# Infini-attention with a SiLU feed-forward layer on one core: constants behind the norms, split transposes, one load on another queue, and a new list of work

## The chip, the cores and the metric

The kernel runs on one core of one Trainium2 chip. The metric is the device time of one execution in microseconds (us), as the median of several runs. The engines are TensorE (PE: matmuls; PEld: its weight loads), VectorE (DVE), ScalarE (ACT), GpSimd (POOL) and SyncE (SP, which here only issues DMAs). "L724" is line 724 of the kernel before.

## The reference

The input x is 2048 x 512, bf16. A layer norm feeds two branches, whose sum is added to x.

```python
xn = layernorm(x)
# A: 32 heads of 16, 4 segments of 512 rows, with a memory M, z carried between them
q, k, v = xn @ wq, xn @ wk, xn @ wv
phi = lambda t: where(t > 0, t + 1, exp(t))
for s in range(4):
    p = softmax(qs @ ks.T * 16**-0.5 + causal mask)
    a_dot = p @ vs
    a_mem = (phi(qs) @ M) / (phi(qs) @ z + 1e-6)
    o = g * a_mem + (1 - g) * a_dot          # g = sigmoid(beta), one per head
    M += phi(ks).T @ vs;  z += sum(phi(ks))
A = concat(o) @ wo
# B: feed-forward, inner width 1792
B = silu(xn @ w1) @ w2
out = x + A + B
```

## The kernel before

Everything runs as one flat program. A string, ORDER, lists 1349 words; a loop at the end of the kernel calls one small function (a "piece") for each word, in this order. Each engine carries out its own instructions in the order in which the words issue them, and waits only where an operand, or a buffer, is not ready. A word names the piece and its indices: `v0.1.2` is part 2 of the value product of segment 0, row tile 1. The list is thus the whole schedule: no loop over tiles or segments sets it.

The x rows come in 16 tiles of 128. The first four are loaded one by one (`load_x`, L158), tiles 0 and 2 from SyncE's queue and 1 and 3 from ScalarE's; the other tiles and the weights follow from SyncE's, except w2 and wo, which `lw0` and `lw1` load from ScalarE's (L169).

The head of the list, for tiles 0 to 3, goes tile by tile. `xc`: VectorE's statistics (L286); `xd`: their mean and variance (L289); `xq`: ScalarE's root (L303); `xi`: VectorE's reciprocal (L306); `Nv`: the normalised tile xn_t (L315); `X`: four transposes on TensorE into one PSUM bank, ptr (`turn_mm`, L845); `Xa`/`Xv`: copies of that bank into xnT by ScalarE or VectorE (`turn_copy`, L851), two copies of two blocks for tiles 0 and 1, one copy for the others. From tile 4 on, `xs` is both statistics, `xg` is root and reciprocal for four tiles on GpSimd (L297, and a power, L300), and `XD` transposes by DMA. `busy44` and `busy6` are matmuls on zeros that keep TensorE running (L864). `tb` loads ScalarE's table for the exponential.

VectorE's constants are words too: `odd` (pm_odd and pm_even, L223, L224), `omask` (L235), `bmask`, and `kind` (five small instructions, L239 to L246). They are needed by the first split of keys (odd), by the first merge of odd heads (omask), by the gate (kind) and by the memory's mask (bmask). Before the list VectorE zeroes zraw (L188) and lows (L262).

Products (`k`, `q`, `v`, `h`, `n`, `o`) accumulate in banks of a pool of four (`bank`, tag "pb"); a copy gives the bank back: `kv`/`ka`, `qv`/`qa`, `vv`/`va` by VectorE or ScalarE, `ha` (ScalarE's tanh, L492) and `hv` (VectorE, L497) for the feed-forward. `product` uses the whole 128x128 array (L336), or four column tiles of 32 (L338) where the next tiled word needs columns.

Attention comes in 72 batches, `S0` to `S71`, 18 for a segment, in the list's own order (S0 S2 S1 S3 S4 S7 S5 S11 S6 ...). A batch is a set of score matmuls into psS, four banks at once, of which there is a single copy (L724); ScalarE's exp out of psS (L730); and GpSimd's causal selects on the weights (L744). The next batch's scores can start only when the exp before has emptied psS. Batches S0 to S4 need the key tiles' split copies: `kf` (VectorE and ScalarE, for the first), `kp` (GpSimd, L385). `E`n and `O`n multiply the weights of column tile n with the values (L791), and need the selects of all their batches: E0 those of S0, S1 and S4. `Ev`/`Ov` copy the result and give back the bank; SyncE then moves the sums of the weights by DMA into zraw. `Om` merges.

`fp` (GpSimd, L417), `fa` (ScalarE) and `fv` (VectorE, L433) make phi of the keys, `gp`, `ga`, `gv` that of the queries. `tanh` (ScalarE, L249) and `gate` make the gate. `o`, `oc`, `od` add up the output, `st` stores it; for the last tile `oh` and `sh` do so in two halves.

Of the kernel before, what the change touches and what calls it, by code (L numbers as in the profile page):

```python
# [19 lines left out]
S1 Nv5 XD5 h0.0.2 h0.0.3 ha0.0 hv0.0 h0.1.0 h0.1.1 fp0.2 h0.1.2 h0.1.3 q0.2.0  # L20
S3 q0.2.1 q0.2.2 q0.3.0 q0.3.1 q0.3.2 q0.2.3 Nv7 qv0.2 ha0.1 h0.2.0 h0.2.1 kp0.2 q0.3.3
S4 qv0.3 hv0.1 XD7 fv0.2 fa0.3 h0.2.2 v0.3.0 v0.3.1 v0.3.2 t0.0 t0.2 xs10 h0.3.0 h0.3.1 h0.3.2 h0.4.0 fp0.3 h0.3.3 ha0.3 v0.3.3
S7 vv0.3 fp0.1 hv0.3 h0.4.1 h0.4.2 h0.4.3 kp0.3 h0.2.3 v1.2.0 ha0.4 v1.2.1 xs13 tanh E0 Ev0
S5 v1.2.2 v1.2.3 h0.5.0 hv0.4 h0.5.1 h0.5.2 ha0.2 h0.5.3 vv1.2 fv0.3 O0 Ov0
S11 lw0 hv0.2 xs11 q1.1.0 q1.1.1 q1.1.2 v1.1.0 v1.1.1 v1.1.2 v1.1.3 q1.1.3 q1.2.0 lw1
S6 vv1.1 q1.2.1 q1.2.2 q1.2.3 v1.3.0 v1.3.1 v1.3.2 qv1.1 ga1.1 xs8 qv1.2 v1.0.0 v1.0.1 xs9 xg8.4 v1.0.2 v1.0.3 vv1.0 v1.3.3 ha0.5 hv0.5 t0.3
S8 h0.6.0 h0.6.1 h0.6.2 gp1.1 h0.6.3 ha0.6 fv0.1 q1.0.0 q1.0.1 q1.0.2 E1
S9 vv1.3 q1.0.3 h0.7.0 h0.7.1 Ev1 hv0.6 h0.7.2 h0.7.3 ha0.7 h0.8.0 h0.8.1 h0.8.2 xs15 k1.3.0
S10 qv1.0 t0.1 hv0.7 k1.3.1 k1.3.2 k1.3.3 kv1.3 h0.8.3 fa1.3 Nv8 O1 Nv10 Ov1 q1.3.0 XD8 ha0.8 hv0.8 k1.2.0 k1.2.1 k1.2.2
S13 q1.3.1 q1.3.2 Nv9 q1.3.3 qv1.3 k1.2.3 Nv11 XD11 h0.9.0 h0.9.1 Om1 h0.9.2 h0.9.3 h0.10.0 ha0.9 hv0.9 kv1.2 kp1.2  # L30
S12 k1.0.0 k1.0.1 h0.10.1 h0.10.2 h0.10.3 k1.1.0 k1.1.1 XD9 k1.0.2 k1.0.3 ha0.10 gv1.1 kv1.0 hv0.10 kp1.0
S15 k1.1.2 h1.0.0 h1.0.1 h1.0.2 k1.1.3 h1.0.3 ha1.0 xs14 E2 kv1.1 XD10 Ev2
S17 O2 Ov2 h1.10.0 h1.10.1 h1.10.2 kp1.1 xl0.2 m0.2 mv0.2 h1.10.3 m0.0 ha1.10 mv0.0 hv1.0 fp1.3
S21 hv1.10 h0.11.0 h0.11.1 h0.12.0 h0.11.2 h0.11.3 h0.12.1 h1.3.0 ha0.11 h0.12.2 h0.12.3
S14 ha0.12 xs12 k2.1.0 hv0.11 Om0 gp1.0 h1.3.1 k2.1.1 kv2.1 hv0.12 q2.1.0 q2.1.1
S16 xg12.4 k2.2.0 k2.2.1 h1.3.2 h0.13.0 qv2.1 kv2.2 h1.3.3 Om2 E3 ha1.3
S19 h0.13.1 hv1.3 h0.13.2 h0.13.3 kp2.2 Ev3 O3 ha0.13 Ov3 v2.1.0 v2.1.1 vv2.1
S24 hv0.13 o0.2.7 oc0.2.10.1 od0.2.11.2 fv1.3 h1.8.0 h1.8.1 Nv15 XD15 h1.8.2 h1.8.3 h1.11.0 h1.11.1 h1.11.2 ha1.8
S18 hv1.8 xl0.0 o0.2.6 h1.11.3 ha1.11 o0.2.8 q2.3.0 q2.3.1 h1.1.0 h1.1.1 Nv14 qv2.3 hv1.11
S22 sv0 h1.1.2 h1.1.3 ha1.1 o0.2.2 k2.0.0 k2.0.1 oc0.2.5.0 od0.2.11.0 o0.0.13 od0.0.0.0  # L40
S20 kv2.0 hv1.1 o0.0.10 v2.2.0 v2.2.1 vv2.2 r0.0 o0.0.11 oc0.0.2.1 t1.3 E4 Ev4 ga1.0 kp1.3
S28 gp1.2 o0.2.3 r0.3 od0.2.11.3 r0.1 od0.0.0.3 r0.2 gate o0.2.1 w0 z0.3 z0.1 h1.7.0 h1.7.1 h1.7.2 h1.7.3 q2.0.0 ha1.7 oc0.0.7.0
S26 hv1.7 z0.0 oc0.0.2.0 o0.0.3 o0.0.8 q2.0.1 z0.2 fa1.1 qv2.0 o0.2.4 o0.0.12 O4
S23 h1.4.0 oc0.0.7.1 o0.2.9 o0.0.6 h1.4.1 o0.0.1 Nv12 Ov4 h1.4.2 h1.4.3 ha1.4 od0.0.0.1 o0.0.4 bmask gv1.0 od0.0.0.2
S25 h1.9.0 h1.9.1 kp2.1 Om3 zv0.3 h1.9.2 XD12 h1.9.3 ha1.9 oc0.2.10.0 hv1.4 o0.2.12 XD14 E5 zv0.1 o0.2.15
S29 xl1.1 Ev5 fp1.1 xl0.3 o0.2.17 o0.2.13 oc0.2.5.1 O5 hv1.9 mw0.0 zv0.0 ga1.2 k2.3.0 Ov5 k2.3.1 kv2.3
S27 o0.0.14 o0.0.15 o0.2.0 h1.2.0 zv0.2 h1.2.1 h1.2.2 h1.2.3 ha1.2 Om4 o0.0.17 hv1.2 o0.0.16
# [28 lines left out]
S57 h2.1.1 ha2.1 o1.1.12 oc1.1.10.0 o1.3.10 oc1.3.3.0 o1.1.11 o1.3.11 gv3.0 o1.1.4 hv2.1 o1.3.15
S54 od1.3.9.0 o1.1.8 ga3.1 o1.3.17 kp3.3 o1.1.0 od1.1.6.2 h3.11.0 o1.3.1 o1.1.2 h3.11.1 st1.3 ha3.11 od1.1.6.3 gp3.3 st1.1 O12 hv3.11
S59 o2.2.11 oc2.2.1.1 gp3.1 E12 fill Ev12 Ov12 dv2.3 h3.7.0 h3.7.1 d2.1 o2.2.2 oc2.2.6.0 ha3.7
S60 o2.0.2 o2.2.5 o2.0.7 h3.12.0 h3.12.1 hv3.7 ha3.12 o2.0.1 dv2.0 n2.0
S62 od2.2.13.1 zv2.0 nv2.0 o2.0.12 oc2.0.5.0 oc2.0.13.0 z2.3 o2.0.9 gv3.1 hv3.12 h3.1.0 h3.1.1 o2.0.10 o2.2.9 ha3.1 z2.1  # L80
# [862 lines left out]
```

## Time and profile before

| | us |
|---|---|
| median of 3 runs | 221.3 (220.81 to 221.44) |
| the profiled execution's own time | 220.8 |
| its span in the trace | 219.1 |
| TensorE busy | 211.6 (97%) |
| ScalarE busy | 184.2 (84%) |
| VectorE busy | 181.0 (83%) |
| GpSimd busy | 126.8 (58%) |

The granted clock of TensorE in the trace is 1.00 from end to end. The span begins shortly before the first instruction and ends with the last DMA of the output; 1.7 us of the profiled execution lie outside it. All times inside the trace are counted from the span's start. In the rows of the timeline the first number is the start, the second the duration; what stands in brackets is how long the engine was idle before, and what ended that. A row "x44" is a group of 44 instructions in a row. In the groups by line the two numbers behind the bar are the time busy in all (us) and the mean of one (ns).

### The profile page before, as it was taken

What the parts mean: (1) busy time and instruction counts of PE and PEld (TensorE: products, weight loads), DVE (VectorE), ACT (ScalarE), POOL (GpSimd) and SP (SyncE); (2) the same over time, 40 slices, a digit from 0 to 9 for tenths busy, and PEclk for the clock granted to TensorE, in tenths of its full rate; (3) what the DMA queues carried; (4) which work ended last, traced back from release to release, by engine and by line L of the source; (5) the groups of instructions that cost most, each with busy time, mean ns of one, the idle gap of its engine ahead of it and who ended that gap; (6) DMA issues with size and microseconds to landing.
All of it is one profiled execution on the core that took longest, in us unless ns stands there. A gap on an engine that the chain in (4) does not pass through costs nothing.

```text
span 219.1 us, 9343 instructions
## 1 busy us (share of the span) xinstructions
PE 211.6 (97%) x4019; PEld 116.3 (53%) x4042; DVE 181.0 (83%) x370; ACT 184.2 (84%) x173; POOL 126.8 (58%) x203
## 2 busy tenths in 40 slices
PE   7999999999999999999999999999999999999994
PEld 7666655556544544445544445455454544465663
DVE  7899999999897878757988979777899798669364
ACT  3899989999999999999999999999999988860000
POOL 6039986679687845695845486667768473410000
PEclk9999999999999999999999999999999999999999
...
GB/s 197 357 372 128 79 129 344 42 79 46 4 4 75 25 86 71 83 62 29 51 74 61 43 121 28 47 79 7 4 99 75 75 76 45 97 60 76 97 52 97
DMA packets 33273, 19.60 MB, mean 89 GB/s; under 512 B 14672, under 2 KB 33232, under 8 KB 33232
## 3 DMA queue, kind: packets, MB, share of 16 engines
q1 hardware_dynamic: 30608, 16.39, 29.1%
...
q14 instruction: 10, 0.08, 0.1%
...
## 4 chain that ended last, share of the span: by engine, by line
PE 82%; DVE 9%; POOL 4%; issue 2%; ACT 1%
PE ps L336 20%; PE psO L338 16%; PE ps L338 15%; PE psS L724 9%; PE psO L336 9%; PE psV L791 8%; PE psS L338 4%; DVE stats L286 2%; POOL Pb L744 2%; DVE Vz L406 1%; POOL k L385 1%; DVE hT L497 1%; DVE pk L433 1%; POOL lows L744 1%; PE ptr L845 1%
## 5 line engine op out<-in xcount | busy, mean ns | idle before, releaser
L730 ACT ACTIVATE Pb<-psS 128x2048 bf16<-128x2048 f32 x72 | 135.2, 1877 | 6.3 <-PE psS L724 4.1
L744 POOL TENSOR_SCALAR_AFFINE_SELECT Pb<-Pb 128x512 bf16<-128x512 bf16 (+2 forms) x88 | 61.6, 710 | 19.2 <-ACT Pb L730 16.5
L497 DVE SCALAR_TENSOR_TENSOR hT<-th,ps 128x512 bf16<-128x512 bf16 x56 | 38.0, 681 | 10.6 <-ACT th L492 10.2
L744 POOL TENSOR_SCALAR_AFFINE_SELECT lows<-Pb 64x512 bf16<-64x512 bf16 (+1 forms) x40 | 23.2, 581 | 37.5 <-ACT Pb L730 31.1
L338 PE MATMUL psO<-w_sb,hT 128*32 128x512 bf16 (+2 forms) x708 | 43.3, 321 | 0.0
L336 PE MATMUL ps<-xnT,w_sb 128*128 128x512 bf16 (+1 forms) x165 | 34.2, 329 | 0.4 <-DVE Vz L406 0.2
L492 ACT ACTIVATE th<-ps 128x512 bf16<-128x512 f32 x56 | 33.2, 594 | 1.7 <-PE ps L338 1.6
L338 PEld LDWEIGHTS <-hT 128*32 128x32 bf16 x876 | 21.6, 97 | 14.0 <-issue 2.6
L338 PE MATMUL ps<-xnT,w_sb 128*32 128x512 bf16 (+1 forms) x448 | 26.4, 348 | 0.0
L724 PE MATMUL psS<-qT,k 32*128 32x64 bf16 (+3 forms) x512 | 23.0, 233 | 0.5 <-ACT Pb L730 0.3
L336 PEld LDWEIGHTS <-w_sb 128*128 128x128 bf16 x168 | 15.8, 98 | 11.4 <-issue 1.0
L791 PE MATMUL psV<-Pb,Vz 128*32 128x448 bf16 (+7 forms) x512 | 21.6, 286 | 0.2 <-POOL Pb L744 0.2
L724 PEld LDWEIGHTS <-k 32*128 32x128 bf16 x512 | 9.4, 92 | 22.8 <-issue 22.2
L336 PE MATMUL psO<-w_sb,hT 128*128 128x512 bf16 (+2 forms) x82 | 20.9, 326 | 0.6 <-issue 0.5
L791 PEld LDWEIGHTS <-Vz 128*32 128x32 bf16 x768 | 16.2, 97 | 9.2 <-issue 0.8
L621 DVE SCALAR_TENSOR_TENSOR o_out<-psO,x_res 128x512 bf16<-128x512 f32 x14 | 9.6, 689 | 6.6 <-PE psO L338 4.9
L338 PEld LDWEIGHTS <-w_sb 128*32 128x32 bf16 x448 | 11.2, 96 | 7.3 <-issue 1.6
L724 PE MATMUL psS<-qT,kT 16*128 16x448 bf16 (+3 forms) x256 | 14.7, 269 | 0.0
L821 DVE CAST oraw<-psV 128x512 bf16<-128x512 f32 x15 | 10.2, 682 | 3.1 <-PE psV L791 3.0
L406 DVE CAST Vz<-ps 128x512 bf16<-128x512 f32 x15 | 10.2, 682 | 2.8 <-PE ps L338 1.6
L336 PEld LDWEIGHTS <-hT 128*128 128x128 bf16 x89 | 7.8, 98 | 8.7 <-issue 2.2
L336 PE MATMUL ps<-xnT,wq_sb 128*128 128x256 bf16 (+1 forms) x59 | 12.1, 322 | 0.2 <-issue 0.2
...
## 6 DMA issues: line engine op xcount, KB each, us to landing
...
```

Of the source, the lines that this page charges most:

```text
L286: nc.vector.bn_stats(out=stats[t][:], in_=xs(t, t + 1)[:, 0, :])
L336: return [nc.tensor.matmul(out, lhsT=lhsT, rhs=rhs, start=start, stop=stop, skip_group_check=True)]
L338: nc.tensor.matmul(out[c : c + 32], lhsT=lhsT[:, c : c + 32], rhs=rhs, start=start, stop=stop, tile_position=(0, c), skip_group_check=True,)
L406: copy(out=Vzs[s % 2][:, j, :, 0:3:2, :], in_=sts[s].pop(("v", j))[:, :].rearrange("p (h r d) -> p h r d", r=2, d=DH),)
L492: nc.scalar.activation(out=th[:], in_=sts[s]["h", ft][:, :], func=AF.Tanh, scale=0.5)
L497: nc.vector.scalar_tensor_tensor(out=st["hT"][:, ft, :], in0=st.pop(("th", ft))[:], scalar=1.0, in1=st.pop(("h", ft))[:, :], op0=ALU.add, ...
L621: out = nc.vector.scalar_tensor_tensor(out=o_out[:], in0=st.pop(("psO", j)), scalar=0.5, in1=st["x", j][:], op0=ALU.mult, op1=ALU.add)
L724: nc.tensor.matmul(psS[:, g, c : c + q2 - q1], lhsT=keys[rows], rhs=st["qT"][rows, dt, q1:q2], start=True, stop=True, tile_position=(32 * ...
L730: exp = nc.scalar.activation(out=blocks(Pb, b).rearrange("p y g c -> p g y c"), in_=psS[:, :, :].rearrange("p g (y c) -> p g y c", c=BLOCK ...
L744: over[id(Pb)].append(nc.gpsimd.affine_select(out=out, in_=in_, compare_op=ALU.is_ge, fill=0.0, base=base, pattern=[[0, out.shape[1]], [1, ...
L791: nc.tensor.matmul(psV[32 * g : 32 * g + 32, q0 : q0 + nq].rearrange("p (y c) -> p y c", y=weights.shape[2]), lhsT=Vzs[s % 2][:, kt, 4 * d ...
L821: copy(out=oraw[:], in_=sts[s].pop(("psV", 0))[:, :])
```

## The change

Four edits, and a new list.

1. The constants move in the list: `odd` behind tile 3's copy, `bmask` ahead of phi of the first key tile, `omask` and `kind` behind S0. Before, kind, odd and omask were its first three words.
2. `turn_mm` and `turn_copy` use two banks for tiles 0 and 1, two transposed blocks in each, so that each copy has a bank of its own. Before, both copies read one bank.
3. Tile 2 of x is loaded from ScalarE's queue. SyncE's issues one load fewer ahead of the weights.
4. The column split of the last tile's two halves is written as a table, LAST_COLS, with the same 256 and 256 columns.
5. The list keeps its words (four copies change engine: kv0.1 becomes ka0.1, qa3.2 and qa3.3 become qv3.2 and qv3.3, Ev14 becomes Ea14), and most stand elsewhere. The batches keep their order. Cut to the code and the first stretches:

```diff
-    load_x(nc.scalar, 1, 1)
-    load_x(nc.sync, 2, 1)
-    load_x(nc.scalar, 3, 1)
+    for t in range(1, TPS):
+        load_x(nc.scalar, t, 1)
...
-        width = D if half is None else D // 2
-        first = 0 if half is None else half * width
+        first, width = (0, D) if half is None else LAST_COLS[half]
...
+    LAST_COLS = ((0, 2 * P), (2 * P, 2 * P))
...
+    def turn_parts(t):
+        return 2 if t < 2 else 1
+
     def turn_mm(t, n):
-        ptr = xn["ptr", t] = bank([P, DT, n, P], BF16, "ptr")
-        for i in range(n):
-            xn_t = xn.pop(t + i)
-            for dt in range(DT):
-                nc.tensor.transpose(ptr[:, dt, i, :], xn_t[:, dt * P : (dt + 1) * P], ident[:])
+        parts = turn_parts(t)
+        size = DT // parts
+        xns = [xn.pop(t + i) for i in range(n)]
+        ptrs = xn["ptr", t] = []
+        for part in range(parts):
+            ptr = bank([P, size, n, P], BF16, "ptr")
+            for i in range(n):
+                for d in range(size):
+                    dt = part * size + d
+                    nc.tensor.transpose(ptr[:, d, i, :], xns[i][:, dt * P : (dt + 1) * P], ident[:])
+            ptrs.append(ptr)
...
```

The list before, to S6:

```
kind odd omask ones0 ones1 zeros xc0 xd0 xc1 xq0 xi0 Nv0 busy44 xd1 xq1 xc2 xi1 X0.1 Nv1 xd2 Xa0.1 busy6 v0.0.0 v0.0.1 xq2 X1.1 Xa1.1 xs3 xi2 Nv2 v0.0.2 xq3 v0.0.3 xi3 v0.1.0 v0.1.1 Nv3 X2.1 va0.0 k0.0.0 k0.0.1 tb Xv2.1 X3.1 v0.1.2 v0.1.3 Xv3.1 vv0.1 k0.1.0 k0.0.2 k0.0.3 ka0.0 fp0.0 kf0.0 q0.0.0 q0.0.1 q0.0.2 q0.0.3 xs4 k0.1.1 qa0.0 k0.1.2 k0.1.3 kv0.1 fa0.0 xs7
S0 k0.3.0 fa0.1 k0.2.0 k0.2.1 k0.2.2 k0.2.3 kv0.2 k0.3.1 k0.3.2 q0.1.0 xs5 xs6 xg4.4 fv0.0 k0.3.3 kv0.3
S2 q0.1.1 v0.2.0 kp0.1 q0.1.2 q0.1.3 qv0.1 v0.2.1 v0.2.2 v0.2.3 vv0.2 fa0.2 Nv6 Nv4 XD6 XD4 h0.0.0 h0.0.1
S1 Nv5 XD5 h0.0.2 h0.0.3 ha0.0 hv0.0 h0.1.0 h0.1.1 fp0.2 h0.1.2 h0.1.3 q0.2.0
S3 q0.2.1 q0.2.2 q0.3.0 q0.3.1 q0.3.2 q0.2.3 Nv7 qv0.2 ha0.1 h0.2.0 h0.2.1 kp0.2 q0.3.3
S4 qv0.3 hv0.1 XD7 fv0.2 fa0.3 h0.2.2 v0.3.0 v0.3.1 v0.3.2 t0.0 t0.2 xs10 h0.3.0 h0.3.1 h0.3.2 h0.4.0 fp0.3 h0.3.3 ha0.3 v0.3.3
S7 vv0.3 fp0.1 hv0.3 h0.4.1 h0.4.2 h0.4.3 kp0.3 h0.2.3 v1.2.0 ha0.4 v1.2.1 xs13 tanh E0 Ev0
S5 v1.2.2 v1.2.3 h0.5.0 hv0.4 h0.5.1 h0.5.2 ha0.2 h0.5.3 vv1.2 fv0.3 O0 Ov0
S11 lw0 hv0.2 xs11 q1.1.0 q1.1.1 q1.1.2 v1.1.0 v1.1.1 v1.1.2 v1.1.3 q1.1.3 q1.2.0 lw1
```

The list after, to S6:

```
ones0 ones1 zeros xc0 xd0 xc1 xq0 xi0 Nv0 busy44 xd1 xq1 xc2 xi1 X0.1 Nv1 xd2 Xa0.1 busy6 X1.1 xq2 v0.0.0 v0.0.1 v0.0.2 Xa1.1 v0.1.0 v0.1.1 xs3 xq3 xi2 Nv2 v0.0.3 X2.1 xi3 Nv3 v0.1.2 X3.1 v0.1.3 Xv2.1 k0.0.0 tb k0.0.1 Xv3.1 odd k0.0.2 vv0.1 va0.0 k0.0.3 ka0.0 kf0.0 q0.0.0 xs4 xs7 q0.0.1 q0.0.2 q0.0.3 k0.1.0 qa0.0 bmask k0.1.1 k0.1.2 fa0.0 fp0.0 fv0.0 t0.0
S0 omask kind k0.2.0 k0.2.1 xs6 xs5 xg4.4 k0.1.3 ka0.1 fp0.1 v0.2.0 v0.2.1 v0.2.2 q0.1.0 q0.1.1 q0.1.2 kp0.1
S2 v0.2.3 fa0.1 k0.2.2 k0.2.3 k0.3.0 k0.3.1 kv0.2 k0.3.2 k0.3.3 q0.1.3 vv0.2 qv0.1 kv0.3 kp0.3 Nv6
S1 h0.0.0 h0.0.1 h0.0.2 h0.0.3 XD6 h0.3.0 ha0.0 v0.3.0 v0.3.1 Nv5 XD5 v0.3.2 h0.1.0
S3 Nv4 h0.1.1 h0.1.2 hv0.0 v0.3.3 vv0.3 h0.3.1 h0.3.2 XD4 h0.3.3 h0.2.0 ha0.3 h0.1.3 xs10 hv0.3
S4 fv0.1 h0.2.1 h0.2.2 q0.3.0 q0.3.1 q0.3.2 q0.3.3 Nv7 q0.2.0 fp0.3 q0.2.1 q0.2.2 q0.2.3 ha0.1 XD7 t0.1 fa0.2 qv0.3
S7 hv0.1 h0.4.0 qv0.2 h0.4.1 h0.4.2 h0.2.3 ha0.2 h0.4.3 kp0.2 xs9 fp0.2 E0 Ev0 v1.2.0
S5 tanh v1.2.1 v1.2.2 hv0.2 xs11 v1.2.3 v1.1.0 v1.1.1 vv1.2 h0.5.0 v1.1.2 v1.1.3 vv1.1 ha0.4 hv0.4 xs8 xg8.4 h0.5.1
S11 h0.5.2 h0.5.3 ha0.5 O0 q1.1.0 Ov0 q1.1.1 q1.1.2 q1.1.3
```

Behind that, lw0 stands behind S6 and lw1 behind S14 (both behind S11 before), and VectorE's Om3, sv0, the recips r0 and w0 stand in the stretches of S18 and S22.

More of the change, by code (lines that the diff above doesn't have):

```diff
@@ L20 @@
[L20 to L47, printed above, removed]
@@ L76 @@
[L76 to L80, printed above, removed]
@@ new lines @@
+S11 h0.5.2 h0.5.3 ha0.5 O0 q1.1.0 Ov0 q1.1.1 q1.1.2 q1.1.3
+S6 k1.2.0 k1.2.1 qv1.1 k1.2.2 ga1.1 hv0.5 lw0 fv0.2 v1.3.0 v1.3.1 q1.2.0 v1.3.2 v1.3.3 vv1.3 k1.2.3 kv1.2 Nv8 XD8 q1.0.0
+S8 Nv10 q1.2.1 q1.2.2 q1.2.3 fa0.3 t0.2 h0.6.0 h0.6.1 h0.6.2 Nv11 q1.0.1 XD11 gate qv1.2 h0.6.3 E1 Ev1 ha0.6 hv0.6
+S9 q1.0.2 h0.8.0 h0.8.1 q1.0.3 k1.0.0 k1.0.1 h0.8.2 h0.8.3 qv1.0 Nv9 XD9 xs14 k1.0.2 k1.0.3 kv1.0 kp1.0 ha0.8
+S10 fv0.3 t0.3 hv0.8 h0.7.0 h0.7.1 h0.7.2 XD10 gp1.1 v1.0.0 v1.0.1 h0.7.3 v1.0.2 v1.0.3 vv1.0 Om0 k1.1.0 ha0.7 hv0.7
@@ new lines @@
+S13 k1.1.1 O1 Ov1 h0.9.0 h0.9.1 h0.9.2 h0.9.3 h0.10.0 ha0.9 xs15
+S12 h0.10.1 h0.10.2 h0.10.3 ha0.10 k1.1.2 k1.1.3 q1.3.0 q1.3.1 q1.3.2 q1.3.3 hv0.9
+S15 h1.0.0 h1.0.1 xs13 kv1.1 h1.0.2 hv0.10 qv1.3 h1.10.0 h1.10.1 xl0.2 E2 Ev2 h1.0.3 ha1.0 hv1.0 h1.10.2 xs12
+S17 h1.10.3 k1.3.0 ha1.10 k1.3.1 k1.3.2 xg12.4 k1.3.3 kv1.3 O2 h0.12.0
+S21 kp1.1 h0.12.1 fp1.3 k2.1.0 h0.12.2 h0.12.3 ha0.12 Ov2 hv1.10 gv1.1 k2.1.1 m0.2 mv0.2 h0.11.0
+S14 lw1 h0.11.1 k2.2.0 k2.2.1 kv2.1 kv2.2 q2.1.0 q2.1.1 hv0.12
+S16 h1.3.0 h1.3.1 h1.3.2 kp1.2 qv2.1 h0.11.2 Om1 h0.11.3 m0.0 mv0.0 h1.3.3 ha1.3 ha0.11 Nv15 E3 Ev3
@@ new lines @@
+S19 h0.13.0 h0.13.1 h0.13.2 hv1.3 h0.13.3 ha0.13 hv0.11 O3 v2.1.0 v2.1.1
+S24 q2.3.0 q2.3.1 mw0.0 Ov3 Nv13 hv0.13 h1.8.0 h1.8.1 h1.8.2 h1.8.3 vv2.1 kp1.3 ha1.8 o0.2.7
+S18 qv2.3 h1.11.0 h1.11.1 h1.1.0 h1.1.1 h1.1.2 Om3 hv1.8 h1.11.2 od0.2.11.2 h1.11.3 ha1.11 fp1.2 od0.2.11.1 sv0 r0.0 oc0.2.10.1 o0.2.4 r0.3
+S22 h1.1.3 k2.0.0 o0.2.2 k2.0.1 hv1.11 XD15 r0.1 kv2.0 o0.2.13 kp2.1 r0.2 w0 ha1.1 hv1.1 z0.2 o0.2.1 o0.0.13 od0.0.0.0 z0.0
+S20 o0.0.6 o0.2.6 v2.2.0 z0.3 v2.2.1 vv2.2 fa1.3 Nv12 XD12 oc0.2.10.0 E4
@@ L663, in half_store @@
     def half_store(h):
-        st, j, cols = sts[LAST], TPS - 1, slice(h * D // 2, (h + 1) * D // 2)
+        first, width = LAST_COLS[h]
+        st, j, cols = sts[LAST], TPS - 1, slice(first, first + width)
         assert len(st.pop(("done", j, h))) == 4 * (FT + DT)
-        o_half = work.tile([P, L], BF16, name="o_half", tag="pos")[:, 0 : D // 2]
+        o_half = work.tile([P, L], BF16, name="o_half", tag="pos")[:, 0:width]
         out = nc.vector.scalar_tensor_tensor(
@@ L838, in odd_merge @@
         )
+    def turn_parts(t):
+        return 2 if t < 2 else 1
     def turn_mm(t, n):
-        ptr = xn["ptr", t] = bank([P, DT, n, P], BF16, "ptr")
-        for i in range(n):
-            xn_t = xn.pop(t + i)
-            for dt in range(DT):
-                nc.tensor.transpose(ptr[:, dt, i, :], xn_t[:, dt * P : (dt + 1) * P], ident[:])
+        parts = turn_parts(t)
[9 more added lines that the diff above has]
+            ptrs.append(ptr)
     def turn_copy(t, n, copy):
-        ptr, parts = xn.pop(("ptr", t)), 2 if t < 2 else 1
-        for i in range(parts):
-            ds = slice(i * DT // parts, (i + 1) * DT // parts)
+        size = DT // turn_parts(t)
+        for part, ptr in enumerate(xn.pop(("ptr", t))):
             copy(
-                out=xnT[:, ds, t * P : (t + n) * P],
-                in_=ptr[:, ds, :, :].rearrange("p d n c -> p d (n c)"),
+                out=xnT[:, part * size : (part + 1) * size, t * P : (t + n) * P],
+                in_=ptr[:, :, :, :].rearrange("p d n c -> p d (n c)"),
             )
```

88 lines of the change are left out of this document (48 added, 40 removed).

## The prediction

> **What bounds the kernel now.** I read the page first (shares, chain), then the chain in order of time, then the timeline of the first 32 us, because the diff touches only the head of the program and the order of the list.
>
> ```profile
> span 219.1 us, 9343 instructions
> PE 211.6 (97%) x4019; PEld 116.3 (53%) x4042; DVE 181.0 (83%) x370; ACT 184.2 (84%) x173; POOL 126.8 (58%) x203
> PE 82%; DVE 9%; POOL 4%; issue 2%; ACT 1%
> L730 ACT ACTIVATE Pb<-psS 128x2048 bf16<-128x2048 f32 x72 | 135.2, 1877 | 6.3 <-PE psS L724 4.1
> PEld L724 <- issue: 22.2, 67, 0.4
> ```
>
> TensorE carries 82% of the chain. The last row, from the waits, is the cost of a score batch: 22.2 us in 67 waits, 0.33 each, before it can load keys again. So the time is the sum of all matmul passes, plus a fixed price for each of 72 batches, plus whatever a late operand adds. One stretch from score batch to score batch, by the windows view (edges put on the first score matmul; the first number after the edges is the length, the next PE's busy time):
>
> ```profile
> 12.07:14.47 2.40, 2.40 (x26) 1.80 (x26) 2.26 (x6) 2.40 (x3) 0.00 (x0) 1.00 1.06 381
> 24.27:26.96 2.69, 2.49 (x66) 1.70 (x66) 2.26 (x6) 2.69 (x4) 2.46 (x5) 1.00 0.52 99
> 29.36:31.96 2.60, 2.48 (x27) 0.91 (x18) 2.56 (x7) 2.29 (x2) 2.15 (x5) 1.00 0.39 96
> 190.76 0.40 PE L724 MATMUL psS<-qT,k 32*128 32x192 bf16 x8
> 209.95 0.39 PE L338 MATMUL ps<-phiQT,Mbf 128*32 128x512 bf16 x4
> 210.17 0.39 PE L338 MATMUL psS<-wo_sb,oT 128*32 128x512 bf16 x4
> ```
>
> The last two rows start 0.22 us apart: one pass of 512 columns, 0.213 to 0.217 (I use 0.213). S0's stretch holds nine passes, 1.92, and takes 2.40, so a batch costs 0.48 beside its passes. S0 to S71 is 190.76 − 12.07 = 178.69 in 71 stretches, 2.517 on average; a stretch with under nine passes still takes about 2.40 (exp 1.88, scores, hand-over). Work put into another stretch is therefore free unless a stretch falls under nine passes, or an operand comes late. Two stretches above lose: S7's (2.69, with 8.5 passes by the list) 0.29, S11's (2.60, nine passes) 0.20.
>
> **The new list as a whole.** By the list both versions hold the same passes, the same ScalarE, VectorE and GpSimd work (two copies change engine in each direction), 144 changes between whole and split arrays, and the same 72 batches in the same order. Counting passes by stretch, old stretches under nine lose 0.83 in all, new ones 0.85 (0.2 each behind S2 and S3, 0.1 each behind S7, S11, S13, S17). The new list has nine passes more before S71 and nine fewer behind it, so S71 comes some 1.9 later without meaning anything for the end. The rewritten column split of the last tile gives the same 256 and 256 columns: nothing.
>
> **The head.**
>
> ```profile
> 0.78 0.90 ACTq L158 DMA_DIRECT2D x_lo<-in_A_x_dram  x2
> 0.79 0.87 SPq L158 DMA_DIRECT2D x_lo<-in_A_x_dram  x2
> 1.10 4.17 PE L864 MATMUL psS<-zraw 128*128 128x128 bf16 x44 [1.10 <-DVE zraw L188]
> 1.40 1.23 DVE L262 MEMSET lows<- 64x1408 uint32 x1 [0.35 <-issue]
> 2.66 0.22 DVE L239 TENSOR_REDUCE kind<-ident 128x1 f32<-128x64 bf16 x1
> 3.48 0.15 DVE L235 CAST omask<-pm_odd 128x1 int32<-128x1 f32 x1
> 3.56 0.68 DVE L286 BATCH_NORM_STATS2 stats<-x_lo 128x6 f32<-128x512 bf16 x1
> 4.55 0.29 ACT L303 ACTIVATE rstd_all<-mv_all,eps 128x1 f32<-128x1 f32 x1 [1.35 <-DVE mv_all L289]
> 5.60 0.40 PE L845 MATMUL ptr<-ident,xn_t 128*128 128x128 bf16 x4 [0.32 <-DVE xn_t L315]
> 9.30 0.42 DVE L851 COPY xnT<-ptr 128x512 bf16<-128x512 bf16 x1 [0.16 <-PE ptr L845]
> 12.07 0.21 PE L724 MATMUL psS<-qT,k 32*128 32x64 bf16 x4 [0.16 <-ACT qT L399]
> q1 hardware_dynamic: 165, 0.16, 17.1%
> q10 hardware_dynamic: 130, 0.12, 13.3%
> DVE ri L560 <- DMA zraw<-odd: 0.4, 1, 0.4
> ```
>
> kind, odd and omask fill VectorE from 2.66 to 3.56 and xc0's statistics follow with no gap. With the constants gone, xc0 could start at 2.63, unless tile 0 of x is later. No row shows its landing. The q rows (DMA view, 0 to 2.7 us) say that 0.28 MB had moved by then on both queues, more than tile 0's 0.13; the last row is VectorE sitting 0.4 until a DMA landed, my nearest row for landing behind movement. So 2.7 + 0.4, about 3.1 to 3.2: gain 0.4, bounds 0 (it landed at 3.56) and 0.93 (at 2.63).
>
> Does 0.4 reach S0? X0 stands behind busy44 on TensorE, over at 1.10 + 4.17 = 5.27; X0 began at 5.60, so it gains at most 0.33. Two banks per tile free X0's first copy two transposes earlier, half of 0.40 less a hand-over, 0.1. But the later path is VectorE's: statistics, norms of tiles 1 to 3, the copy at 9.30, then keys, queries and S0 (12.07). That moves by the 0.4; X1 ahead of v0.0.0 costs nothing, as TensorE still waits for norms (that cover gone, v0.0.0 starts one block of transposes, 0.40, later). I take S0 0.4 earlier, 11.67, with one pass (0.21) fewer done before it. Moving tile 2's load makes ScalarE's queue issue a third one, 0.90/2 = 0.45 more, where its table load is queued behind; that has until the first root, 4.55 before and some 4.15 now, and whatever doesn't fit falls on X0 whole; SP's weights issue 0.43 sooner, counted zero, since both queues moved at once in the q rows. The Trainium skill speaks against that edit ("DMA: Bandwidth & Descriptors", section "Issuing engines are not separate DMA queues"): DMAs from any issuer interleave on the same 16 engines, only issue time is saved. The two q rows, running side by side, agree; by a rule of independent queues tile 2 would land sooner, yet it is needed only after tile 1's statistics.
>
> **From S0 to S5: GpSimd.** What S0 gains must get past the selects.
>
> ```profile
> 15.13 0.66 DVE L286 BATCH_NORM_STATS2 stats<-x_hi 128x6 f32<-128x512 bf16 x1
> 15.93 0.69 DVE L433 SCALAR_TENSOR_TENSOR pk<-ex,pos 128x512 bf16<-128x512 bf16 x1
> 11.30 0.69 DVE L286 BATCH_NORM_STATS2 stats<-x_hi 128x6 f32<-128x512 bf16 x1
> 16.10 0.57 POOL L297 TENSOR_SCALAR rstd_all<-mv_all 128x4 f32<-128x4 f32 x1 [0.45 <-DVE mv_all L289]
> 23.32 1.02 POOL L385 TENSOR_SCALAR k<-kT,pm_odd 128x512 bf16<-128x512 bf16 x1
> 25.59 1.09 POOL L744 TENSOR_SCALAR_AFFINE_SELECT Pb<-Pb 128x1024 bf16<-128x1024 bf16 x1
> 26.73 0.29 PE L791 MATMUL psV<-Pb,Vz 128*32 128x256 bf16 x4 [0.20 <-POOL Pb L744]
> ```
>
> In the chain GpSimd runs without a break from 16.10 (the power for tiles 4 to 7) to 26.69, where S4's select lets E0's last four matmuls go. The new list puts the same GpSimd work before S4's select, in another order: power, fp0.1, kp0.1, S2, kp0.3, S1, S3, S4 (old: power, S2, kp0.1, S1, fp0.2, S3, kp0.2, S4), so 10.59 again. It starts when all four statistics of tiles 4 to 7 are in. Tile 4's statistics stood at 11.30 behind the first key tile; they move by at most the head's 0.4, and only if x_hi has landed by then, which no row shows: 10.9 to 11.3, I take 11.0. From there VectorE does four statistics at 0.80 (15.93 − 15.13), fv0.0 0.69, kind 0.64 of the 0.90 between 2.66 and 3.56, omask and bmask some 0.2: 15.7, and the power stands, with a hand-over, at 15.9 (15.7 to 16.2) instead of 16.10. E0's end and S5 come 0.2 earlier (26.75 for 26.95), not 0.4.
>
> **From S5 on.**
>
> ```profile
> 24.90 1.87 ACT L730 ACTIVATE Pb<-psS 128x2048 bf16<-128x2048 f32 x1
> 27.13 0.21 ACT L249 ACTIVATE gate<-beta_r 128x1 f32<-128x1 bf16 x1
> 27.41 1.88 ACT L730 ACTIVATE Pb<-psS 128x2048 bf16<-128x2048 f32 x1
> 29.84 0.68 DVE L828 CAST odd<-psV 128x512 bf16<-128x512 f32 x1
> 30.57 1.02 PE L336 MATMUL ps<-wv_sb,xnT 128*128 128x512 bf16 x4
> ```
>
> The tanh of the gate was hidden in S7's stretch by E0's wait; now it stands behind S5, with an exp and ha0.4. Exp, ha and tanh took 27.41 − 24.90 = 2.51, so 0.11 over 2.40 (bounds 0 and tanh's whole 0.21). S11's lost 0.20 was v1.1's bank, given back by Ov0 at 30.52; it goes, but v1.3.0 now asks for a bank behind Ov0 in S6, after a VectorE stretch of six pieces in S5: I keep half of it, −0.10.
>
> **Sum against the profiled execution** (220.8, span 219.1, 1.7 outside it; the median 221.3 lies 0.5 above): S5 −0.20, the pass owed +0.21, tanh +0.11, bank −0.10, short stretches behind S5 (0.33 for 0.30) +0.03: +0.05. On the median's scale 221.3, own range 220.9 to 221.8. No change: the head's gain is eaten by GpSimd and by the pass not yet done. A measurement of this kernel tells some 0.3% (0.66 us) from none.
>
> **Rivals.**
> *Faster: GpSimd is not in the way.* If its chain is 5% shorter (kp's odd half took 1.02 at 23.32 and 0.69 elsewhere) or tile 0 lands near 2.7, S0's gain passes E0, whose wait goes too. From the sum: −0.4 −0.29 for −0.20 gives −0.44; with a head of 0.6, −0.64. For: only 0.20 of idle stands at 26.73. Against: the same instructions in a row. About 220.6.
>
> *Slower: the selects queue later.* kp0.1 and kp0.3 now stand ahead of the selects of S2 and S1, and kp0.2, that S11 needs, stands behind S4's and S7's selects and fp0.3.
>
> ```profile
> L385 POOL TENSOR_SCALAR k<-kT,pm_odd 128x512 bf16<-128x512 bf16 x15 | 11.5, 766 | 1.0
> L417 POOL TENSOR_SCALAR pos<-kT 128x512 bf16<-128x512 bf16 x12 | 7.7, 646 | 7.2 <-ACT kT L376 6.8
> L744 POOL TENSOR_SCALAR_AFFINE_SELECT Pb<-Pb 128x512 bf16<-128x512 bf16 x32 | 21.1, 660 | 11.1 <-ACT Pb L730 10.0
> ```
>
> From 26.5: fp 0.65, select 0.66, odd half 0.77 to 1.02, four hand-overs 0.3: 28.9 to 29.1, while S11's slot is 26.75 + 2.40 = 29.15. It decides once S4's select ends after about 26.7: each 5% on GpSimd's 10.59 adds 0.5 to E0's wait, and S11 then waits as well. 0.5 + 0.3 + 0.05: about 222.2. Here the Trainium skill has a rule ("SBUF — State Buffer", section "Who interferes with whom"): a VectorE instruction with two SBUF inputs contends with a GpSimd one that reads SBUF. No row here isolates it; fv's and kp's spread (1.02 against 0.77) would fit.
>
> *The head gives nothing.* Tile 0 landed at 3.5, or X0 stays behind the keep-warm matmuls: S0 at about 12.0, the power at 15.9 to 16.1, E0 as before; S5 0 for −0.20. 221.5. The skill's "TensorE: Matmul & The Clock Gate" (Part 1) warms the array over a free-running window of about 3.4 us, so busy44's end may itself move; this one execution's 4.17 for 44 cannot show it.
>
> **Numbers.** Forecast 0.33, faster rival 0.27, slower rival 0.27, empty head 0.13. Faster by over 0.3%: 0.20 + 0.04; slower: 0.23 + 0.03 + 0.03; the rest, 0.47, within. The range takes half a rival's spread on both sides: 220.3 to 222.5, with some 0.08 left out below and 0.09 above.
>
> **What would show it.** Right: xc0 at about 3.15, S0 at 11.6 to 11.7, the power near 15.9, E0's last matmuls released by S4's select at about 26.5 with an idle of 0.4 to 0.6 before them, S11 within 0.1 of 29.2, S71 near 192.5. Wrong: S0 later than 11.9; no GpSimd release at E0; a wait for kp0.2 at S11; a new wait over 0.3 between S24 and S22, where VectorE's pieces are now bunched.

## The result: slower by 1.2%

| | before | after |
|---|---|---|
| median of 6 runs each | 221.25 us (220.79 to 221.44) | 223.86 us (223.00 to 224.66) |
| ratio | | 1.012, interval 1.0091 to 1.015 |
| once more, in a later group | 221.2 | 223.22 (222.66 to 224.54), 1.009, interval 1.006 to 1.012 |
| profiled execution, span | 220.8, 219.1 | 223.0, 221.3 |

The forecast was 221.3 with 220.3 to 222.5 around it: the direction and the size were wrong. The runs of after are spread over 1.7 us, those of before over 0.65; the profiled execution of after is the fastest of its six. Sizes below are taken from 223.5, the median of all twelve runs of after, and those under 0.3 us mean little beside this spread. Its page, from the top and from the chain:

```profile
span 221.3 us, 9307 instructions
PE 213.4 (96%) x3999; PEld 117.7 (53%) x4024; DVE 180.7 (82%) x370; ACT 184.7 (83%) x173; POOL 127.9 (58%) x203
PE 75%; ACT 8%; DVE 8%; POOL 6%; issue 2%; DVEq 0%; POOLq 0%
PEld L724 <- issue: 20.9, 65, 0.4
```

TensorE's share of the chain fell from 82% to 75%: more of the time now belongs to others. A batch's own price is what it was (20.9 us in 65 waits, 22.2 in 67 before). A stretch from batch to batch is taken to need 0.48 and 0.213 for each pass, but at least 2.40, as in the prediction; what it takes longer is its loss. By the first score matmul of each batch, the 2.2 us of span that after has more lie mainly in three places: S0 stands at 12.84 instead of 12.07 (+0.77); the stretches between S20 and S41 lose 1.3, where before loses nothing; and from S71 to the end of the last instruction after takes 26.83 for 22.61 us of passes, before 28.32 for 24.42 (+0.32 beside the passes). One pass more, 0.21, is left to do behind S0. Against that, S7 and S11 lose 0.13 and 0 instead of 0.29 and 0.20.

The head of after, timeline:

```profile
0.79 1.41 ACTq L158 DMA_DIRECT2D x_lo<-in_A_x_dram  x3
1.10 4.87 PE L872 MATMUL psS<-zraw 128*128 128x128 bf16 x44 [1.10 <-DVE zraw L187]
3.25 0.69 DVE L285 BATCH_NORM_STATS2 stats<-x_lo 128x6 f32<-128x512 bf16 x1 [0.62 <-DMA x_lo<-in_A_x_dram]
5.77 0.63 PE L853 MATMUL ptr<-ident,xn_t 128*128 128x128 bf16 x4
6.23 0.65 ACT L859 COPY xnT<-ptr 128x256 bf16<-128x256 bf16 x2 [0.56 <-PE ptr L853]
6.43 0.66 DVE L285 BATCH_NORM_STATS2 stats<-x_lo 128x6 f32<-128x512 bf16 x1
8.10 1.28 ACT L308 ACT_TABLE_LOAD   x1
9.50 0.57 ACT L405 CAST Vz<-ps 128x512 bf16<-128x512 f32 x1
10.12 1.03 PE L335 MATMUL ps<-xnT,wk_sb 128*128 128x256 bf16 x8 [0.63 <-ACT Vz L405]
12.84 0.21 PE L724 MATMUL psS<-qT,k 32*128 32x64 bf16 x4 [0.16 <-ACT qT L398]
```

Tile 0's statistics stand at 3.25, after a wait for the load: the 0.3 of the constants is there. It is gone again at X0, the first transposes: they started at 5.77, right behind the 44 matmuls on zeros and without a wait for the norm, and before at 5.60. More is lost at 10.12: the first key product waits 0.63 for ScalarE's copy of v0.0, and starts 0.05 after it ends. The four banks had gone to v0.0, v0.1, X2 and X3, and by what ended the wait it is v0.0's that the product takes. The copy runs at 9.50, behind the table load of 8.10. In the list before, va0.0 stands ahead of tb, and the copy ran at 8.06.

### The profile page after: what moved, and what is told of

It reads as the page before. It is cut to its first block, busy times and chain, and to the rows that moved or that the text cites. A ratio compares the mean times of both kernels' runs of the same rounds, so it can differ in the third digit from the quotient of the medians.

```text
span 221.3 us, 9307 instructions
## 1 busy us (share of the span) xinstructions
PE 213.4 (96%) x3999; PEld 117.7 (53%) x4024; DVE 180.7 (82%) x370; ACT 184.7 (83%) x173; POOL 127.9 (58%) x203
## 4 chain that ended last, share of the span: by engine, by line
PE 75%; ACT 8%; DVE 8%; POOL 6%; issue 2%; DVEq 0%; POOLq 0%
PE ps L335 17%; PE ps L337 14%; PE psO L337 14%; PE psO L335 9%; PE psS L724 9%; PE psV L791 6%; ACT Pb L730 5%; PE psS L337 3%; POOL Pb L744 3%; PE psS L872 2%; POOL k L384 2%; DVE hT L496 2%; ACT th L491 1%; POOL lows L744 1%; DVE Vz L405 1%
## 5 line engine op out<-in xcount | busy, mean ns | idle before, releaser
L337 PE MATMUL psO<-w_sb,hT 128*32 128x512 bf16 (+2 forms) x628 | 39.5, 333 | 0.0
L335 PE MATMUL ps<-xnT,w_sb 128*128 128x512 bf16 (+1 forms) x142 | 32.0, 337 | 0.3 <-DVE qT L398 0.2
L337 PE MATMUL ps<-xnT,w_sb 128*32 128x512 bf16 (+1 forms) x528 | 29.2, 336 | 0.1
L335 PE MATMUL psO<-w_sb,hT 128*128 128x512 bf16 (+2 forms) x106 | 24.2, 308 | 0.6 <-issue 0.3
L724 PEld LDWEIGHTS <-k 32*128 32x128 bf16 x512 | 9.7, 92 | 22.2 <-issue 20.9
L335 PEld LDWEIGHTS <-w_sb 128*128 128x128 bf16 x148 | 13.2, 98 | 11.7 <-issue 2.4
L337 PEld LDWEIGHTS <-w_sb 128*32 128x32 bf16 x528 | 13.6, 96 | 8.1 <-issue 2.2
L335 PEld LDWEIGHTS <-hT 128*128 128x128 bf16 x109 | 10.0, 98 | 10.3 <-issue 1.4
L335 PE MATMUL ps<-xnT,wk_sb 128*128 128x256 bf16 (+1 forms) x59 | 12.8, 322 | 0.8 <-ACT Vz L405 0.6
L828 DVE CAST odd<-psV 128x512 bf16<-128x512 f32 x15 | 10.3, 684 | 3.3 <-PE psV L791 3.3
L416 POOL TENSOR_SCALAR pos<-kT 128x512 bf16<-128x512 bf16 x12 | 8.1, 681 | 8.0 <-ACT kT L375 7.6
```

The lines of the kernel that those rows point to most:

```text
L335: return [nc.tensor.matmul(out, lhsT=lhsT, rhs=rhs, start=start, stop=stop, skip_group_check=True)]
L337: nc.tensor.matmul(out[c : c + 32], lhsT=lhsT[:, c : c + 32], rhs=rhs, start=start, stop=stop, tile_position=(0, c), skip_group_check=True,)
L416: nc.gpsimd.tensor_scalar(out=pos[:], in0=phi_src(s, of, dt), scalar1=3.0e38, scalar2=0.0, op0=ALU.min, op1=ALU.max)
L724: nc.tensor.matmul(psS[:, g, c : c + q2 - q1], lhsT=keys[rows], rhs=st["qT"][rows, dt, q1:q2], start=True, stop=True, tile_position=(32 * ...
L828: copy(out=odd[:], in_=sts[s].pop(("psV", 1))[:, :])
```

## The experiments

Three were possible causes of the late head (the copy behind the table load, the moved load, the split banks), one was proposed by the trace for the middle, one for the end. All runs below are medians beside before on the same chip; a difference from after is taken from 223.5, on other chips, where no run of after is named beside it.

**One copy moved.**

```diff
-... Xv2.1 k0.0.0 tb k0.0.1 Xv3.1 odd k0.0.2 vv0.1 va0.0 k0.0.3 ...
+... Xv2.1 va0.0 k0.0.0 tb k0.0.1 Xv3.1 odd k0.0.2 vv0.1 k0.0.3 ...
```

> The kernel after, with one word moved: the copy va0.0 stands ahead of the table load tb and of k0.0.0. Theory (in the head the key product's bank hangs on va0.0, which ScalarE reaches only after the 1.28 us table load): k0.0.0 starts at about 9.5 instead of 10.12, S0 at 12.2 to 12.4 instead of 12.84, and the time falls by 0.4 to 0.6 us, to about 223.3. Rival (the head is late because TensorE's clock came up later: 44 keep-warm matmuls in 4.87 us instead of 4.17): S0 stays within 0.15 of 12.84 as long as the 44 take 4.87, and the time stays.

222.55 (before 221.16; 1.0058, interval 1.0039 to 1.0077), 0.9 less. The 44 keep-warm matmuls took 4.88 again, k0.0.0 began at 9.46 and S0 stood at 12.29: the copy's place it is, not the clock.

**The same on the kernel before**, the other way round: va0.0 behind tb.

> The kernel before, with one word moved: va0.0 stands behind the table load tb. Theory (bank of va0.0): k0.0.0 starts at about 10.2 instead of 8.42, S0 at 12.7 to 12.9 instead of 12.07, time 0.3 to 0.8 us longer, 221.6 to 222.0 (part of it may vanish in E0's wait for GpSimd). Rival (clock): S0 12.07, time as before, 221.25.

221.49 (1.0015, interval 1.0004 to 1.0026), S0 at 12.60 instead of 12.07. The price at S0 is 0.1 below the forecast, the time 0.1 below its range, and the place is another one: k0.0.0 kept its 8.42 (it did not have to wait for this copy's bank), and tile 3's transposes waited, 9.20 instead of 8.87, then the products behind them. The copy behind the table load costs in both lists; which product pays depends on the bank.

**The code without the list, and the load alone.**

```diff
-    load_x(nc.sync, 2, 1)
+    load_x(nc.scalar, 2, 1)
```

> The changed code (two banks for tiles 0 and 1, tile 2 of x from ScalarE's queue, the table of columns) under the list of before. Theory (the loss lies in the list): S0 within 0.3 us of 12.07 and a time within 0.5 us of 221.25. Rival (the split banks or the moved load make the head late): S0 at 12.6 or later, time 221.8 or more.

> The kernel before with one edit: tile 2 of x is loaded from ScalarE's queue, one bank per tile as before. Theory (tile 3 lands late): VectorE waits 0.3 to 0.9 us for x_lo ahead of tile 3's statistics, S0 at 12.4 to 13.0, time 0.1 to 0.4 us over that of before, as with both code edits. Rival (the late head of the changed code comes from the split banks): no wait for x_lo over 0.1, S0 within 0.15 of 12.07.

The two medians are 221.38 (1.0013, interval 1.0001 to 1.0026) and 221.44 (1.001, interval 0.9994 to 1.0027), both with runs up to 222.2 and 222.7. My theory for the first was wrong in its S0: 12.97, not within 0.3 of 12.07. The load alone does it (12.76). In the median it costs only 0.1 in this list, inside its interval: the runs of before are spread as well (220.79 to 221.90 on that chip), and its own profile, at 220.8, is one of the fastest. Timeline rows of VectorE, of the load alone, of after with the end changed (below), and of after with the load put back:

```profile
7.43 0.70 DVE L285 BATCH_NORM_STATS2 stats<-x_lo 128x6 f32<-128x512 bf16 x1 [0.58 <-DMA x_lo<-in_A_x_dram]
```
```profile
7.99 0.69 DVE L285 BATCH_NORM_STATS2 stats<-x_lo 128x6 f32<-128x512 bf16 x1 [1.31 <-DMA x_lo<-in_A_x_dram]
13.99 0.21 PE L724 MATMUL psS<-qT,k 32*128 32x64 bf16 x4 [0.16 <-ACT qT L398]
```
```profile
6.73 0.66 DVE L286 BATCH_NORM_STATS2 stats<-x_lo 128x6 f32<-128x512 bf16 x1
```

These are the statistics of tile 3. It is now the third load of ScalarE's queue and leaves behind weights that SyncE issues 0.45 sooner. VectorE waits for it not at all in the two profiles of after, and 0.29, 0.58, 0.67, 0.83 and 1.31 in the other five with the load on that queue; never in the ten with tile 2 on SyncE's. S0 follows: 12.70 in the second profile of after without the wait, 13.99 with 1.31. The DMA view shows the transfer itself: the packets of ScalarE's queue end at 3.9 in before with its two tiles, and in the seven profiles with three tiles at 5.4 (after) to 7.6 (after with the end changed); where VectorE waits, the statistics begin 0.3 to 0.4 later.

**The load put back in after.**

> The kernel after, with the load of tile 2 back on SyncE's queue; the rest as after. Theory (as the third load of ScalarE's queue, behind weights that SyncE issues earlier, tile 3 of x lands 1.5 to 3.4 us later than before, by a different amount in every run): VectorE no longer waits for x_lo ahead of tile 3's statistics, S0 at 12.4 to 12.6, the median falls by 0.4 to 0.9 us to about 223.2, and the runs lie within 0.8 us of each other instead of 1.7. Rival (only the table load ahead of va0.0 makes the head late, the load is hidden): S0 at 12.8, time within 0.3 us of 223.86.

222.66 (222.36 to 223.5; 1.0066, interval 1.0044 to 1.0088), 0.8 less, S0 12.70 and not 12.4 to 12.6, the runs within 1.1 and not 0.8. The second profile of after, where tile 3 came in time, has S0 at 12.70 as well: what the moved load costs in this list is seen in the medians and in the profiles with a wait. The 44 matmuls took 3.92 here, the shortest of all, and S0 was still 0.6 late: the clock is not the cause.

**Both repairs of the head**, beside after once more.

> The kernel after, nothing changed, beside the runs of this group, so that sizes can be compared on one chip. Theory (tile 3 lands late by a different amount in every run): median 223.3 to 224.2, spread over 1 us, and in the profile a wait of VectorE for x_lo ahead of tile 3 of 0 to 1.3 us with S0 later by about as much.

> The kernel after with both repairs of the head, tile 2 on SyncE's queue and va0.0 ahead of the table load. Theory (both faults feed the same S0, and what is won there beyond some 0.5 us is taken by E0's wait for GpSimd, which the list makes start at the same time): S0 at 11.9 to 12.2, S7's stretch longer by 0.2 to 0.4, time 222.2 to 222.6, hardly better than with either alone. Rival (the two add): 221.3 to 221.6.

After 223.22, with both repairs 222.07 (1.005, interval 1.003 to 1.007): 1.15 less on one chip, 1.4 from 223.5. S0 stood at 12.08, that of before. The time lies 0.1 below my range and 0.5 above the rival's, but my mechanism is not in the profile: S7's stretch lost 0.12, as in after (0.13), and not 0.2 to 0.4 more, so GpSimd took nothing. At S0 the two add (12.70 − 12.08 = 0.62 for the copy, and tile 3's wait as it falls); in the time the single repairs gave 0.9 and 0.8, and both together 1.2 to 1.4. Whether they add there, the spread doesn't let one say.

**The middle.** In after's chain of waits GpSimd carries the time from 90.2 to 104.0 almost without a break, and in the timeline its queue around S41 reads:

```profile
102.03 0.69 POOL L384 TENSOR_SCALAR k<-kT,pm_odd 128x512 bf16<-128x512 bf16 x1
102.70 0.48 POOL L384 TENSOR_SCALAR k<-kT,pm_even 128x256 bf16<-128x256 bf16 x1
103.13 0.83 POOL L744 TENSOR_SCALAR_AFFINE_SELECT Pb<-Pb 128x512 bf16<-128x512 bf16 x1
104.02 0.62 PE L791 MATMUL psV<-Pb,Vz 128*32 128x448 bf16 x16 [0.41 <-POOL Pb L744]
```

The select that O7's matmuls need stands behind a key split (kp2.3) that no batch needs before S49. The new list has kp2.2 and kp2.3 in S33 and S35; kp2.0 and three pieces of phi stand between S31 and S34 as well. The edit:

```diff
-S33 ... o0.1.15 kp2.2 st0.0 E6          -S35 ... o0.1.0 kp2.3 qv2.2 ...
+S36 gp2.2 k3.1.1 kp2.2 q3.3.0 ...       +S40 ... od1.2.1.0 kp2.3
```

> The kernel after, with two words moved: the GpSimd key splits kp2.2 and kp2.3, which no batch needs before the second pair of segment 2, go from the stretches of S33 and S35 to those of S36 and S40. Theory (between S20 and S41 the kernel after loses 1.3 us, most of it because GpSimd's selects queue behind these pieces): the loss of S32, S34 and S41 (0.16, 0.22, 0.61) goes, the time falls by 0.7 to 1.1 us, to 222.8 to 223.2. Rival (the losses there are banks given back late by VectorE): time within 0.3 us of 223.86.

222.87 (1.008, interval 1.0063 to 1.0097), 0.6 less. The losses of S34 and S41 (0.22 and 0.61) are gone, that of S32 is not (0.18, against my theory), and S43 has a new one, 0.38.

**The end.** In after st3.2, 0.68 on VectorE, stands between the two half stores:

```profile
217.20 0.42 DVE L668 SCALAR_TENSOR_TENSOR o_half<-psS,x_res 128x256 bf16<-128x256 f32 x1 [0.55 <-PE psS L337]
217.54 0.68 DVE L620 SCALAR_TENSOR_TENSOR o_out<-psS,x_res 128x512 bf16<-128x512 f32 x1
218.14 0.41 DVE L668 SCALAR_TENSOR_TENSOR o_half<-psS,x_res 128x256 bf16<-128x256 f32 x1
218.25 0.33 SPq L625 DMA_DIRECT2D out_dram<-o_out  x1
218.68 0.39 SPq L672 DMA_DIRECT2D out_dram<-o_half  x1
```

The last half's store waits for VectorE until 218.14 and for SyncE until 218.68. The edit moves four half products and sh0 behind st3.2.

```diff
-oh14.0 oh15.0 o3.2.13 o3.2.4 oh5.0 o3.2.8 oh13.1 o3.2.12 o3.2.6 o3.2.17 sh0 st3.2 oh5.1
+o3.2.13 o3.2.4 o3.2.8 o3.2.12 o3.2.6 o3.2.17 st3.2 oh14.0 oh15.0 oh5.0 oh13.1 sh0 oh5.1
```

> The kernel after with the end of the list changed: the store st3.2 of row tile 2 stands ahead of four of the last half products and of sh0, instead of between sh0 and the last seven half products; the same matmuls. Theory (VectorE's 0.68 us for st3.2 and SyncE's issue of its store hold up the last half sh1): the span behind the last matmul falls by 0.3 to 0.5 us, time about 223.4 to 223.6. Rival (the end is set by the matmuls alone): time within 0.15 us of 223.86.

223.51 (1.0094, interval 1.0075 to 1.0114). From S71 to the end 26.50 instead of 26.83: the 0.32 that after has over before beside the passes. The median says nothing: the spread of after's head is larger than the effect.

**All four together, and the key splits twice more.**

> The kernel after with all four repairs: tile 2 on SyncE's queue, va0.0 ahead of the table load, kp2.2 and kp2.3 later, st3.2 earlier; constants, split banks and the rest of the new list as they are. Theory (the four causes are all there is, and partly add up): S0 at 11.7 to 12.0, time 220.6 to 221.4, that is within 0.3% of before. Rival (the new list has other losses that show once these are gone): 221.8 or more.

221.65 (1.0016, interval 1.0002 to 1.0029): between the two forecasts; of the 2.3 us between 223.5 and before, 1.9 are undone. S0 stood at 12.07 and not at 11.7 to 12.0, and S43 still lost 0.38.

> The kernel after with the four repairs, and kp2.3 moved once more, from the stretch of S40 to that of S45. Theory (the stretch of S43, which lost 0.38 us once kp2.3 stood ahead of it, loses it to GpSimd: E8's last matmuls wait for a select): the loss of S43 goes, no other appears up to S49, time 221.1 to 221.4. Rival (S43's loss comes from something else in the new list): S43 still loses 0.3 us, time 221.65.

221.69: the rival's numbers came, S43 lost 0.38 again, and S47 a new 0.24. I had moved the wrong piece. GpSimd's queue in that run, and what E8 waited for:

```profile
110.02 0.61 POOL L417 TENSOR_SCALAR pos<-qT 128x512 bf16<-128x512 bf16 x1
110.72 0.69 POOL L385 TENSOR_SCALAR k<-kT,pm_odd 128x512 bf16<-128x512 bf16 x1
111.39 0.48 POOL L385 TENSOR_SCALAR k<-kT,pm_even 128x256 bf16<-128x256 bf16 x1
111.94 0.66 POOL L745 TENSOR_SCALAR_AFFINE_SELECT lows<-Pb 64x512 bf16<-64x512 bf16 x1
112.67 1.09 POOL L745 TENSOR_SCALAR_AFFINE_SELECT Pb<-Pb 128x1024 bf16<-128x1024 bf16 x1
113.81 0.29 PE L792 MATMUL psV<-Pb,Vz 128*32 128x256 bf16 x4 [0.21 <-POOL Pb L745]
```

S40's exp was over at 109.33 + 1.88 = 111.21; its select began at 111.94, behind gp2.2 and kp2.2, the split that I had put into S36.

> The kernel after with the four repairs, kp2.3 in the stretch of S40 as in the first version of all four, and kp2.2 moved from the stretch of S36 to that of S39. Theory (the last trace shows S40's select starting 0.7 us after its exp, behind gp2.2 and kp2.2, and E8's last matmuls released by that select: the queue is the cause, the piece was the other one): the loss of S43 falls from 0.38 to 0.1 or less, nothing new over 0.15 up to S49, time 221.2 to 221.5. Rival (E8 is late by something else): S43 loses 0.3 again, time 221.65.

221.32 (1.0014, interval 1.0003 to 1.0026). S43's loss is gone. Beside before on their own chips this version is 0.2 slower and the first with all four 0.3. From the other side:

> The kernel before with two words moved: kp2.2 and kp2.3 stand in the stretches of S33 and S35, as in the list after (S19 and S48 before). Theory (GpSimd's selects queue behind them): stretches between S33 and S41, without loss in the kernel before, lose 0.3 to 0.8 us in all, time 221.4 to 222.0. Rival (the loss in the kernel after is tied to the rest of its list): no loss, time within 0.15 us of before.

224.61 (1.0154, interval 1.0134 to 1.0175): 3.5 us, far more than either theory had, and nearly all of it in one stretch, S41's, that took 6.1 us instead of 2.46. Timeline, and windows (the number after TensorE's count is its granted clock):

```profile
103.04 0.66 POOL L744 TENSOR_SCALAR_AFFINE_SELECT Pb<-Pb 128x512 bf16<-128x512 bf16 x1
103.74 0.85 PE L791 MATMUL psV<-Pb,Vz 128*32 128x448 bf16 x16 [2.13 <-POOL Pb L744]
```
```profile
102.00:103.00 1.00, 0.00 (x0) 1.00 0.02 3
104.00:107.40 3.40, 3.40 (x76) 0.50 0.01 1
107.40:108.00 0.60, 0.60 (x40) 1.00 0.00 0
```

O7 waited 2.13 for S34's select, which stood behind kp2.0, kp2.2 and kp2.3; and right after this idle time TensorE's clock was granted at 0.50 for 3.4 us. The wait costs 2.1, the slow clock behind it most of the rest. The executions bear this out: four of the five had a mean granted clock of 0.992 and took 224.59 to 224.98, and the fifth, at 0.999, took 223.48.

**What part of the change is a gain.** The constants alone, and with the split banks, in the list before:

```diff
-kind odd omask ones0 ... Xv3.1 vv0.1 ...         -... gp1.1 ... fv0.1 q1.0.0 ...    -S22 sv0 ...
+ones0 ...            Xv3.1 odd vv0.1 ...          +... fv0.1 omask q1.0.0 ...        +S22 kind sv0 ...
```

> The kernel before with the constants alone moved: odd behind tile 3's copy, omask behind fv0.1, kind ahead of sv0; code and the rest of the list as before. Theory (tile 0 lands at 3.25 to 3.55, so the norms gain 0 to 0.3 us, and S0 as much): S0 at 11.75 to 12.05, time 220.9 to 221.25. Rival (my step in the prediction, 0.4 us at S0): S0 at 11.6 to 11.7, time 220.8. Rival on the other side (the constants cost where they now stand): over 221.5.

> The kernel before with the constants moved and, besides, two banks each for the transposes of tiles 0 and 1; tile 2 of x stays on SyncE's queue. Theory (the first copy starts up to 0.1 us sooner, S0 hardly moves as VectorE's norms set it): within 0.15 us of the kernel with the constants alone. Rival (four banks for two tiles leave the pool of four empty, so v0.0 or X2 waits for a copy): S0 later by 0.3 us or more, time 0.3 us longer.

220.91 (0.9979, interval 0.9964 to 0.9995) and 220.90 (0.9987, interval 0.9972 to 1.0002), before 221.2. Tile 0's statistics began at 3.57 and 3.40 in the two profiles, over the twelve profiles with the constants moved at 3.25 to 3.57, each time after a wait for the load. So VectorE's norms gain 0 to 0.3, depending on the load. S0 gained nothing in either profile: 12.37, against my 11.75 to 12.05, where the first key product waited for its weights until 8.74 (8.42 before), and 12.06, where X0 started at 5.78 behind the matmuls on zeros. With split banks ScalarE's first copy followed X0 by 0.31 instead of 0.44, and the time does not show it. Both medians lie 0.3 below that of before, the first clear of its interval; through which step they do, these profiles don't show.

## Why the prediction was wrong

**The moved load: failed.** I counted the queue that tile 2 left and the tile itself ("needed only after tile 1's statistics"), and not the one behind it on the queue that it joined. "SP's weights issue 0.43 sooner, counted zero" was the term. Tile 3 became third, and cost 0 to 1.3 us at S0 from run to run: S0 stood at 12.70 to 13.99 in the four profiles with after's head. The rule that I weighed there was right, and I drew too little from it. The Trainium skill ("DMA: Bandwidth & Descriptors", section "Issuing engines are not separate DMA queues") says that all issuers' DMAs interleave on the same engines, only issue time is saved. The runs agree: SyncE's weights were issued 0.45 sooner, the third tile 0.45 later, and its last packets moved at 5.4 to 7.6 instead of 3.9.

**The head's path: failed.** I had VectorE's norms carry their gain to S0. In the four profiles with both repairs tile 0's statistics began at 3.27 to 3.48 (3.56 before), and S0 stood at 12.02 to 12.08 (12.07 before): nothing arrived. X1 ahead of v0.0.0 was not free: v0.0.0 started at 6.88 to 6.95 instead of 6.46, the 0.40 of my own bracket and a little more, and ScalarE's copy of v0.0 had to wait for it. Behind that copy ScalarE has the table load and the copy of the first keys, with no idle between them. With all four repairs:

```profile
8.43 0.58 ACT L406 CAST Vz<-ps 128x512 bf16<-128x512 f32 x1 [0.57 <-PE ps L336]
9.03 1.28 ACT L309 ACT_TABLE_LOAD   x1
10.43 0.57 ACT L376 CAST kT<-ps 128x512 bf16<-128x512 f32 x1
```

So S0 hangs on v0.0 and ScalarE's queue, which I did not follow. In the profile of after the matmuls on zeros held X0 as well (5.77), the condition that I had given to the rival with the empty head. And in the list as it came the copy stood behind the table load: S0 12.70 with the load repaired, 12.08 with both. tb ahead of va0.0 was in the list to be read, and so were four tiles for four banks ahead of k0.0.0.

**Tile 0's landing: the mechanism right, mis-sized.** Forecast 3.1 to 3.2, measured 3.25 to 3.57.

**S0 to S5: right in sum, by luck.** I put the power at 15.9; in the four profiles with both repairs it came at 16.13 to 16.38, since S0 had not moved and tile 4's statistics, put at 11.0, began at 11.32 to 11.56, twice after a wait for x_hi. From the power to the end of S4's select I took 10.59, and it took 10.0: the 5% of my faster rival. E0's matmuls then show no wait for GpSimd, which I had named as a sign of being wrong. The two errors cancel: S5 at 26.79 to 26.87 for my 26.75. kp0.2 came in time for S11, and S11's bank and the tanh cost nothing: both bounds at their good end.

**Everything behind S11: failed, by omission.** I summed GpSimd's work up to S4's select, then took "the same GpSimd work" for the rest of the list. The slower rival named the mechanism, selects queueing behind splits, but put it between S4 and S11; it sat between S33 and S41. The same count that I made for 16 to 27 us, stretch by stretch over the list, would have shown kp2.0, kp2.2 and kp2.3 with phi's pieces in S27 to S35.

**The end: not in the prediction.** I had the order sh0, st3.2, sh1 before me and no term for it: 0.32.

**What stands of the sum.** The passes, the score price and the pass owed: over S20 to S33 and S43 to S71 the stretches of after follow the law within some 0.2 each. Two counts were off without weight in the sum: 8.5 passes moved ahead of S71 and not nine, and the stretches under nine passes lose 1.28 in the old list and 1.23 in the new one, not 0.83 and 0.85. Of the 2.2 us in the profiles, 0.77 is the head, 0.32 the end, 0.21 the pass. Of the middle, S34 and S41 (0.83) are shown to be GpSimd's; S13, S16, S20, S29, S32 and S38 lose 0.12 to 0.19 each in every version of the new list. The old list loses nearly as much in other places: over all stretches 0.87 in the profile with constants and split banks, 1.04 in the best version of the new list, which with the pass is about what their spans differ by (219.0 and 219.3). In S20 and S29 a weight load of TensorE waits 0.3 to 0.4 for VectorE; in the other four no wait for an engine stands out. None of these was tried, and their cause stays open, and so does the part of after's spread that remains with tile 2 on SyncE's queue (221.8 to 223.82 with the head repaired).
